# A linear-attention and feed-forward kernel: whole-width weight slices, attention in halves of 64 tokens, values and state at one stride per head

## The chip, the cores and the metric

The kernel runs on one core of a Trainium2 chip, in one launch. The metric is device time in microseconds. The times before are three runs: 548.47, 548.35 and 547.65, median 548.35.

A core has engines that work side by side, each through its own queue and in its own order: PE (TensorE, matrix products, with PEld for its weight loads), DVE (VectorE), ACT (ScalarE) and POOL (GpSimd), for work on elements, and SP (SyncE), which here issues every DMA transfer. Results of PE land in PSUM, everything else is in SBUF, both with 128 partitions.

## The reference

Two steps. A gated linear attention (batch 4, 8 heads, 768 tokens, head width 48) keeps a 48x48 state per head and decays its rows token by token. Its output goes through a feed-forward layer (384 to 2048 to 384) with a hard-swish gate.

```python
for t in range(S):
    state = alpha[:, :, t, :, None] * state + np.einsum('bhd,bhe->bhde', k[:, :, t], v[:, :, t])
    y[:, :, t] = np.einsum('bhd,bhde->bhe', q[:, :, t], state)
...
x = y.transpose(0, 2, 1, 3).reshape(B * S, H * D)
h = x @ w_in
relu6 = np.clip(h + 3.0, 0.0, 6.0)
g = h * relu6 / 6.0
return g @ w_out
```

All arithmetic is in fp32. The weights arrive as float64, and the kernel makes fp32 of their bits.

## The kernel before

**Chunks.** The 3072 tokens are 24 chunks of 128, six for each sequence; NC is 6, and chunk j is the last of its sequence if j % 6 is 5. Heads go in four pairs: head 2p in rows 0-47 and head 2p+1 in rows 64-111 of a tile with the head width in the partitions. For each chunk:

- Load alpha, k and q (L270) and v (L289). Chunks 0-5 are loaded by token and turned by PE (L306). Later ones are loaded in 32-row blocks and turned by DVE's 32x32 block transposes (`by_blocks`, L317), into Q_t and K_t, width in the partitions.
- `decay` (L336) and `growth` (L348) are two DVE scans along the chunk. They yield the factors by which k and q are multiplied (`scaled`, L356), so that scores and state need no further decay inside the chunk.
- `scores` (L401) are k times q per head. Chunks 0-7 compute the full 128x128 square (L408), later ones three of its four 64x64 blocks (L383, L385). `masked` (L411, L388) multiplies them with the triangle on DVE and leaves A_t in SBUF.
- `within` (L518) multiplies values with masked scores into y: 16 products of 128 columns (L539), or from chunk 8 on two times 16 of 64 columns (L529, L533), for which `keep_v` (L396) copies part of the values into a tile v0 on ACT.
- `across` (L543) adds state times q: 12 products of 128 columns (L549), none in the first chunk of a sequence. The state is stored as 128 x 4 x 96, where a head's 48x48 block fills half of the width and zeros the rest.
- `decayed_state` (L468) multiplies the state with the chunk's decay on POOL. `update` (L475) computes k times v over the chunk's tokens, and `next_state` (L499) adds it on DVE, one instruction for each half of the partitions.
- `update` needs k by token. Up to chunk 7 PE turns it back (L423). Later `turn_k` (L447) transposes 32x32 blocks on DVE, `write_k` (L457) writes them to DRAM in one transfer, and `read_k` (L461) reads them back in four, one for each block of 32 tokens. Last chunks do none of it.
- `keep_x` (L554) copies y from PSUM, as the feed-forward's input.

**Groups.** The feed-forward works on 12 groups of two chunks. Its first product is 20 block products for each group from 2 on (`product1`, L685, four 128x128x128 matmuls each), with sums of blocks made by DVE (L627) before and after, and plain matmuls for groups 0 and 1 (L566, L575). ACT copies results (L697) and computes the gate's clip (L586), DVE multiplies (L589). The second product is 7 block products of eight matmuls of 192 columns (`product`, L778) for groups 1 to 11, and plain for group 0 (L604).

**Weights.** `load_weight` (L172) brings eight slices of w_in, each in four transfers of 32 partitions (L184), and eight of w_out in one transfer each. ACT, DVE and POOL turn the bits into fp32 (L204 to L239).

**Order.** Nothing is scheduled by the compiler. A long list of words (L842) is run in order, and each word appends its instructions to its engines' queues; for instance `sc.9.1.2` is the scores of chunk 9 in PSUM banks 1 and 2, `M.4.8` product 8 of group 4. An engine takes its instructions in that order, and waits only for operands and buffers. PSUM has four banks for attention and four for the feed-forward. The words that come up below: `sc` scores, `m` masked, `yi` within, `yx` across, `u` update, `sm` next_state, `st` decayed_state, `kt`/`kw`/`kr` turn, write and read keys, `vh` keep_v, `cy` keep_x, `M`/`P` the block products, `z` warm-up matmuls.

Of the kernel before, what the change touches and what calls it, by code (L numbers as in the profile page):

```python
# [17 lines left out]
def kernel(  # L18
# [32 lines left out]
    nc = tc.nc  # L51
# [10 lines left out]
    GT = G * C  # L62
    W = C + 1
# [3 lines left out]
    HB = C // 2  # L67
# [10 lines left out]

    tri = consts.tile([C, 3, HB], mybir.dt.bfloat16, tag="tri")
    nc.gpsimd.memset(tri, 1.0)  # L80
    for n, b in ((0, 0), (0, 1), (2, 0), (1, 1)):
        at = slice(HB * b, HB * b + HB)
        nc.gpsimd.tensor_copy(out=tri[at, n], in_=mask[at, at])

    v0 = consts.tile([C, H, 64], FP, tag="vfirst", name="vfirst")
    nc.gpsimd.memset(v0, 0.0)
# [9 lines left out]
    for r in range(max(NR, NV)):  # L96
        for name, pad, n in (("a", 1.0, NR), ("k", 0.0, NR), ("q", 0.0, NR), ("v", 0.0, NV)):
            if r >= n:
                continue
            if name == "v":  # L100
                t = consts.tile([C, H, 64], FP, tag=f"v{r}", name=f"v{r}")
            else:
                t = rings[:, 3 * r + "akq".index(name)]
            eng = nc.vector if r == 0 else nc.gpsimd
            if name == "v":
                t4 = t.rearrange("s (p a) e -> s p a e", a=2)
                eng.memset(t4[:, :, 0, D:64], pad)
                eng.memset(t4[:, :, 1, 0 : 64 - D], pad)
            else:
                eng.memset(t[:, :, D:64], pad)  # L110
            ring[name, r] = t
# [16 lines left out]
    st, sm = [], []  # L128
    for r in range(2):
        t = consts.tile([C, NP, 2 * D], FP, tag=f"st{r}")  # L130
        nc.gpsimd.memset(t, 0.0)
        st.append(t)
    for r in range(2):
        t = consts.tile([C, NP, 2 * D], FP, tag=f"sm{r}")
        nc.gpsimd.memset(t, 0.0)
        sm.append(t)
# [35 lines left out]
    def load_weight(i):  # L172
        u = 2 if wide else 1
        dst = weight_dst(i)
        m = dst.shape[1]
        to = raw_of(i).rearrange("p (m n) w -> p m (n w)", m=m) if wide else dst
        if i < NW1:
            n = NSL // KT
            src = moe_w_in[:, u * i * n : u * (i + 1) * n].rearrange(
                "(p t r) f -> p r t f", p=NP, t=KT)  # L180

            for p in range(NP):
                queue = nc.sync
                queue.dma_start(out=to[32 * p : 32 * p + 32], in_=src[p])  # L184
        else:
            o = (i - NW1) * m * C
            nc.sync.dma_start(
                out=to, in_=moe_w_out[o : o + m * C, :].rearrange("(f p) n -> p f n", p=C))
# [45 lines left out]
    def add_low(i):  # L234
# [9 lines left out]
    bank_t = [ps.tile([C, NP, C], FP, tag=f"t{i}", name=f"t{i}_ps") for i in range(4)]  # L244
    Rs, Qs, Ks, kbs, As = (
        [consts.tile([C, *shape], FP, tag=f"{name}{r}", name=f"{name}{r}") for r in range(2)]
        for name, shape in (("R", (NP * W,)), ("q", (NP, C)), ("k", (NP, C)), ("kb", (NP, C)),
                            ("A", (H, C))))
    Ps = consts.tile([C, NP * W], FP, tag="P", name="P")

    def bank(name, j, i):
        ps_t[name, j] = bank_t[i]
        return ps_t[name, j]
# [35 lines left out]
    def load_v(j, z):  # L289
        v_t[j] = ring["v", z]  # L290
        to = v_t[j].rearrange("s (p a) e -> s p a e", a=2)
        sv = rows(v, j).rearrange("(p a) s d -> s p a d", a=2)
        if j >= SWAP:
            for b in range(2):
                for g in range(2):
                    at = slice(HB * (b ^ g), HB * (b ^ g) + HB)
                    for a in range(2):
                        e = (64 - D) * a
                        nc.sync.dma_start(
                            out=to[HB * b : HB * b + HB, 2 * g : 2 * g + 2, a, e : e + D],  # L300
                            in_=sv[at, 2 * g : 2 * g + 2, a])
            return
        nc.sync.dma_start(out=to[:, :, 0, 0:D], in_=sv[:, :, 0])
        nc.sync.dma_start(out=to[:, :, 1, 64 - D : 64], in_=sv[:, :, 1])
# [65 lines left out]
    SWAP = 8  # L370

    def score_blocks(t):
        return t.rearrange("s p r -> s (p r)")[:, 0 : 2 * 3 * HB].rearrange(
            "s (x n t) -> s x n t", x=2, n=3)

    def scores_of_halves(j, *at):
        sc = [bank("sc%d" % o, j, at[o]) for o in range(2)]
        for h in range(H):
            p, a = divmod(h, 2)
            r, g = slice(64 * a, 64 * a + D), p // 2  # L380
            to = score_blocks(sc[a])[:, p % 2]
            k, q = K_t[j][r, p], Q_t[j][r, p]
            nc.tensor.matmul(to[HB * g : HB * g + HB, 0 : 2 + g : 1 + g], k[:, 0:HB],  # L383
                             q.rearrange("r (n t) -> r n t", n=2), start=True, stop=True)
            nc.tensor.matmul(to[HB * (1 - g) : HB * (2 - g), 1 + g], k[:, HB:C], q[:, HB:C],  # L385
                             start=True, stop=True)

    def masked_halves(j):  # L388
        A_t[j] = As[j % 2]
        for o in range(2):  # L390
            nc.vector.tensor_tensor(
                out=score_blocks(A_t[j][:, NP * o : NP * (o + 1)]),
                in0=score_blocks(ps_t.pop(("sc%d" % o, j))),
                in1=tri.unsqueeze(1).to_broadcast([C, 2, 3, HB]), op=ALU.mult)

    def keep_v(j):  # L396
        for b in range(2):
            at, h = slice(HB * b, HB * b + HB), slice(NP * b, NP * b + NP)
            nc.scalar.copy(out=v0[at, h], in_=v_t[j][at, h])

    def scores(j, *at):  # L401
        if j >= SWAP:
            return scores_of_halves(j, *at)

        sc = [bank("sc%d" % o, j, at[o]) for o in range(2)]
        for h in range(H):
            r = slice(64 * (h % 2), 64 * (h % 2) + D)
            nc.tensor.matmul(sc[h % 2][:, h // 2], K_t[j][r, h // 2], Q_t[j][r, h // 2],  # L408
                             start=True, stop=True)

    def masked(j):  # L411
        if j >= SWAP:
            return masked_halves(j)
        A_t[j] = As[j % 2]
        for o in range(2):
            nc.vector.tensor_tensor(
                out=A_t[j][:, NP * o : NP * (o + 1)], in0=ps_t.pop(("sc%d" % o, j)),
                in1=mask.unsqueeze(1).to_broadcast([C, NP, C]), op=ALU.mult)
# [4 lines left out]
    def k_by_token(j, i=None):  # L423
        if not last(j):
            t = bank("kb", j, i)
            for p in range(NP):
                if j < SWAP or p < 2:
                    nc.tensor.transpose(t[:, p], K_t[j][:, p], ident)
                    continue
                for b in range(2):  # L430
                    nc.tensor.transpose(t[HB * b : HB * b + HB, p],
                                        K_t[j][:, p, HB * (1 - b) : HB * (2 - b)], ident)

    def keep_k(j):
        if not last(j):
            kb_t[j] = kbs[j % 2]
            nc.scalar.copy(out=kb_t[j], in_=ps_t.pop(("kb", j)))
# [9 lines left out]
    def turn_k(j):  # L447
        to = k_in_blocks(j).rearrange("r (v p c) -> r p v c", v=V, p=NP)
        src = K_t[j].rearrange("r p (v s) -> r p v s", v=V)
        if j < SWAP:  # L450
            nc.vector.transpose(out=to, in_=src)
            return
        nc.vector.transpose(out=to[:, 0:2], in_=src[:, 0:2])
        for v in (0, 2):
            nc.vector.transpose(out=to[:, 2:4, v : v + 2], in_=src[:, 2:4, 2 - v : 4 - v])

    def write_k(j):  # L457
        far_t[j] = far.tile([C, NP * C], FP, tag="far", name="far")
        nc.sync.dma_start(out=far_t[j], in_=k_in_blocks(j))

    def read_k(j):  # L461
        kb_t[j] = kbs[j % 2]
        to = kb_t[j].rearrange("s p r -> s (p r)").rearrange("s (o w) -> s o w", o=V)
        src = far_t.pop(j).rearrange("(o s) (v w) -> v s o w", s=BLK, v=V)
        for n in range(V):
            nc.sync.dma_start(out=to[BLK * n : BLK * (n + 1)], in_=src[n])

    def decayed_state(j):  # L468

        if j % NC:  # L470
            nc.gpsimd.tensor_tensor(  # L471
                out=st[j % 2], in0=sm[j % 2],
                in1=R_t[j][:, :, 0:1].to_broadcast([C, NP, 2 * D]), op=ALU.mult)

    def update(j, i=None):  # L475
        if last(j):
            return
        u = bank("u", j, i).rearrange("r p n -> r (p n)")[:, 0 : NP * 2 * D].rearrange(
            "r (p n) -> r p n", p=NP)
        ps_t["u", j] = u  # L480
        vs = v_t[j]
        if j >= FAR:
# [529 lines left out]
```

## Time and profile before

The profiled execution took 547.54 us, and its span, from the first to the last instruction, is 545.8 us. The mean granted TensorE clock was 0.999.

| | busy us | share of the span | instructions |
|---|---|---|---|
| PE | 537.1 | 98% | 6222 |
| DVE | 476.9 | 87% | 822 |
| ACT | 202.9 | 37% | 358 |
| POOL | 51.9 | 10% | 76 |

| kind of DMA transfer | number | KB each | median us from issue to landing |
|---|---|---|---|
| w_in slice | 24 and 8 | 192 | 6.2 and 7.5 |
| w_out slice | 8 | 768 | 5.0 |
| keys to DRAM | 13 | 256 | 2.4 |
| keys from DRAM | 52 | 64 | 2.0 |
| v, from chunk 8 on | 128 | 24 | 2.2 |
| v, before | 16 | 96 | 3.1 |

How to read it: an engine's busy time is the union of its instructions' spans. On PE several small matmuls run at once in parts of the array, and the ends of matmuls are modelled, so for PE the starts tell more than the durations. An fp32 matmul stands in the trace as two records. The page's second part cuts the span into 40 slices and gives each a digit, the busy share in tenths. The order of time lists start, duration, engine, line, operation, tiles and shape; "x32" are 32 instructions put together.

### The profile page before, as it was taken

The page shows a single profiled execution, that of the slowest core. Times are in us where ns is not written, and L with a number is a line of the kernel's source. Part 1 is how long each engine was busy: PE and PEld are TensorE (multiplying, and loading weights), DVE is VectorE, ACT ScalarE, POOL GpSimd, SP SyncE. Part 2 cuts the span into 40 slices and gives each one's busy share as a digit, 9 for nine tenths or more (in the row PEclk, how much of TensorE's full clock was granted, in tenths as well). Part 3 has the DMA queues.
Part 4 walks back from the last instruction along what each step waited for, and adds up shares of the span by engine and source line. Part 5 has one row for each costly group of instructions (what it writes and reads, how often), then busy time and mean ns, then how long its engine had stood idle before and what let it go on. Part 6 is the DMA issues. An engine that isn't in the chain of part 4 may idle for free.

```text
span 545.8 us, 14868 instructions
## 1 busy us (share of the span) xinstructions
PE 537.1 (98%) x6222; PEld 511.3 (94%) x6222; DVE 476.9 (87%) x822; ACT 202.9 (37%) x358; POOL 51.9 (10%) x76
## 2 busy tenths in 40 slices
PE   8999999999999999999999999999999999999997
PEld 8888977789899999999999999999999999999996
DVE  7989989999999999999999999999899796465471
ACT  2666664003443342353233233333334332342330
POOL 3333334200000000000000000000000200000000
PEclk9999999999999999999999999999999999999999
DMA  9996677140433552343535342335353110000001
GB/s 182 210 222 127 203 228 186 41 121 17 89 88 81 151 154 49 85 121 89 136 83 154 98 100 49 84 89 157 73 132 95 44 23 16 8 3 23 23 0 37
DMA packets 98515, 52.82 MB, mean 97 GB/s; under 512 B 51472, under 2 KB 91664, under 8 KB 98448
## 3 DMA queue, kind: packets, MB, share of 16 engines
q1 hardware_dynamic: 98448, 51.87, 38.9%
q8 instruction: 49, 0.80, 0.6%
q14 instruction: 18, 0.15, 0.1%
HBM read 43.71 MB, written 8.13 MB: 95 GB/s over the span
## 4 chain that ended last, share of the span: by engine, by line
PE 78%; DVE 12%; DMA 5%; SPq 3%; issue 1%; ACT 0%; POOL 0%; DVEq 0%; POOLq 0%
PE m_ps L796 32%; PE m_ps L693 30%; PE m_ps L571 3%; DMA raw<-in_moe_w_in_dram 2%; PE t_ps L549 2%; PE t_ps L383 2%; PE t_ps L529 1%; PE m_ps L625 1%; SPq L284 1%; PE t_ps L533 1%; DMA g_sb<-in_moe_w_in_dram 1%; DVE g_sb L740 1%; PE t_ps L314 1%; DVE rings L740 1%; PE t_ps L488 1%
## 5 line engine op out<-in xcount | busy, mean ns | idle before, releaser
L699 ACT COPY g_sb<-m_ps 128x512 f32<-128x512 f32 x110 | 63.8, 585 | 158.9 <-PE m_ps L693 130.5
L796 PE MATMUL m_ps<-w,g_sb 128*128 128x192 f32 x704 | 121.7, 326 | 0.0
L796 PEld LDWEIGHTS m_ps<-w,g_sb 128*128 128x128 f32 x704 | 113.8, 190 | 0.6 <-issue 0.2
L796 PE MATMUL m_ps<-rings,g_sb 128*128 128x192 f32 x528 | 91.3, 326 | 0.7 <-DVE rings L740 0.7
L796 PEld LDWEIGHTS m_ps<-rings,g_sb 128*128 128x128 f32 x528 | 85.3, 190 | 1.3 <-issue 1.3
L693 PE MATMUL m_ps<-xc,w 128*128 128x128 f32 x640 | 83.9, 277 | 0.1
L693 PEld LDWEIGHTS m_ps<-xc,w 128*128 128x128 f32 x640 | 77.9, 192 | 2.4 <-issue 1.0
L587 ACT ACTIVATE r<-g_sb,half 128x512 f32<-128x512 f32 x80 | 56.7, 722 | 56.3 <-DVE g_sb L630 18.4
L591 DVE SCALAR_TENSOR_TENSOR g_sb<-r,g_sb 128x512 f32<-128x512 f32 x80 | 53.8, 691 | 7.4 <-ACT r L587 7.3
L693 PE MATMUL m_ps<-xT,raw 128*128 128x128 f32 x400 | 51.8, 276 | 0.0
L471 POOL TENSOR_TENSOR t<-t,R 128x384 f32<-128x384 f32 x20 | 18.5, 926 | 331.7 <-DVE t L509 202.9
L693 PEld LDWEIGHTS m_ps<-xT,raw 128*128 128x128 f32 x400 | 48.5, 192 | 0.4
L740 DVE TENSOR_TENSOR g_sb<-g_sb 128x512 f32<-128x512 f32 (+1 forms) x55 | 44.2, 835 | 0.7 <-PE m_ps L796 0.5
L693 PE MATMUL m_ps<-xT,w 128*128 128x128 f32 x320 | 41.5, 276 | 0.0
L693 PEld LDWEIGHTS m_ps<-xT,w 128*128 128x128 f32 x320 | 39.1, 192 | 0.2
L341 DVE TENSOR_TENSOR_SCAN R<-t,ones 128x516 f32<-128x516 f32 x24 | 31.0, 1292 | 4.0 <-ACT t L332 2.9
L630 DVE TENSOR_TENSOR g_sb<-g_sb 128x512 f32<-128x512 f32 x40 | 27.1, 689 | 7.4 <-ACT g_sb L699 7.4
L571 PE MATMUL m_ps<-xT,w 128*128 128x256 f32 x144 | 32.2, 380 | 1.0 <-POOL w L238 1.0
L693 PE MATMUL m_ps<-xc,raw 128*128 128x128 f32 x240 | 32.2, 277 | 0.0
L571 PEld LDWEIGHTS m_ps<-xT,w 128*128 128x128 f32 x144 | 27.0, 190 | 5.1 <-POOL w L238 1.4
L352 DVE TENSOR_TENSOR_SCAN P<-t 128x516 f32<-128x516 f32 x24 | 30.7, 1279 | 0.2
L693 PEld LDWEIGHTS m_ps<-xc,raw 128*128 128x128 f32 x240 | 29.7, 192 | 0.7 <-issue 0.4
(121 smaller groups left out, 734.8 us busy)
## 6 DMA issues: line engine op xcount, KB each, us to landing
raw<-in_moe_w_out_dram SPq DMA_DIRECT2D x8, 768.0 KB, 5.0
raw<-in_moe_w_in_dram SPq DMA_DIRECT2D x24, 192.0 KB, 6.2
out_dram<-oh SPq DMA_DIRECT2D x44, 96.0 KB, 1.8
kq<-in_k_dram SPq DMA_DIRECT2D x36, 96.0 KB, 2.4
aq<-in_alpha_dram SPq DMA_DIRECT2D x36, 96.0 KB, 2.4
qq<-in_q_dram SPq DMA_DIRECT2D x36, 96.0 KB, 2.5
far<-kq SPq DMA_DIRECT2D x13, 256.0 KB, 2.4
kb<-far SPq DMA_DIRECT2D x52, 64.0 KB, 2.0
```

Of the source, the lines that this page charges most:

```text
L341: nc.vector.tensor_tensor_scan(out=reverse(R, n - 1, n), data0=reverse(ax, n, n), data1=reverse(ones, n, n), initial=0.0, op0=ALU.mult, op ...
L352: nc.vector.tensor_tensor_scan(out=P_t[j], data0=aX[j % 2][:, 0:n], data1=ini[j % 2], initial=0.0, op0=ALU.mult, op1=ALU.add)
L383: nc.tensor.matmul(to[HB * g : HB * g + HB, 0 : 2 + g : 1 + g], k[:, 0:HB], q.rearrange("r (n t) -> r n t", n=2), start=True, stop=True)
L471: nc.gpsimd.tensor_tensor(out=st[j % 2], in0=sm[j % 2], in1=R_t[j][:, :, 0:1].to_broadcast([C, NP, 2 * D]), op=ALU.mult)
L571: nc.tensor.matmul(h[:, f], w1[:, kk, o : o + C], xT_t[g][:, kk], start=(kk == 0), stop=(kk == KT - 1))
L587: nc.scalar.activation(out=to, in_=h, func=AF.Relu, bias=half, scale=1.0 / 6.0)
L591: nc.vector.scalar_tensor_tensor(out=to, in0=r, scalar=1.0, in1=h, op0=ALU.min, op1=ALU.mult)
L630: eng.tensor_tensor(out=out, in0=in0, in1=in1, op=ALU.add if s1 > 0 else ALU.subtract)
L693: nc.tensor.matmul(acc[g][i][:, f * C : (f + 1) * C], spots[w][:, f * C : (f + 1) * C], x_of(g, x), start=(first and f == 0), stop=last, s ...
L699: nc.scalar.copy(out=slots[z], in_=acc[g][i])
L740: nc.vector.tensor_tensor(out=out, in0=in0, in1=in1, op=ALU.subtract)
L796: nc.tensor.matmul(to[g], a, rhs[:, f], start=(first and f == 0), stop=(last and f == HF - 1), skip_group_check=True)
```

## The change

It has these parts; the list of words is written anew throughout.

1. `load_weight`: a w_in slice comes in one transfer of 128 partitions. Which row of w_in lies in which partition changes, and `y_of` places y accordingly.
2. Attention in halves of 64 tokens. Scores are only the two 64x64 blocks on the diagonal. The second half sees the first through the state: there is a state in the middle of a chunk, `half_st`.
3. Values lie in a tile of 128 x 2 x 8 x 64, half b of the tokens in its own 64 partitions; into the other 64 partitions of the same half `place_state` copies the state with two ACT copies (or POOL zeros, at the start of a sequence). Masked scores lie in `As` in the same way, and `place_q` copies q beside them with two ACT copies. `attend` then multiplies both in one product of 128 rows. `within`, `across`, `keep_v` and the tiles v0 and tri go.
4. The state is 128 x 4 x 48. `update` runs in halves, also for the first half of last chunks, so their keys are turned and read back too.
5. `turn_k` is one transpose; `write_k` makes four transfers, with 32-element runs in DRAM in such an order that each of the four of `read_k` reads 2 KB per token in one piece.

Words per kernel: `kt`, `kw`, `kr` 13 to 16, `u` 20 to 24, `sm` 20 to 44 (one instruction each now), `vh` 16 to 0, `qa` (place_q) and `sv` (place_state) 0 to 48, `ya` and `yb` (attend) 24 each for `yi` and `yx`. The words of the feed-forward and of the weights keep their numbers.

```diff
-            src = moe_w_in[:, u * i * n : u * (i + 1) * n].rearrange(
-                "(p t r) f -> p r t f", p=NP, t=KT)
-            for p in range(NP):
-                queue = nc.sync
-                queue.dma_start(out=to[32 * p : 32 * p + 32], in_=src[p])
+            nc.sync.dma_start(out=to, in_=moe_w_in[:, u * i * n : u * (i + 1) * n].rearrange(
+                "(t p) f -> p t f", p=C))
...
+        v_t[j] = vs[z]
+        src = rows(v, j).rearrange("h s d -> s h d")
+        for b in range(2):
+            at = slice(HB * b, HB * b + HB)
+            nc.sync.dma_start(out=v_t[j][at, b, :, 0:D], in_=src[at])
...
+    def scores(j, *at):
+        sc = ps_t["sc", j] = [banks[i][:, 0 : NP * HB].rearrange("s (p t) -> s p t", p=NP)
+                              for i in at]
+        for p in range(NP):
+            for b in range(2):
+                half = slice(HB * b, HB * b + HB)
+                for a in range(2):
+                    r = slice(64 * a, 64 * a + D)
+                    nc.tensor.matmul(sc[a][half, p], K_t[j][r, p, half], Q_t[j][r, p, half],
+                                     start=True, stop=True)
+
+    def masked(j):
+        A_t[j] = As[j % 2]
+        sc = ps_t.pop(("sc", j))
         for b in range(2):
+            half = slice(HB * b, HB * b + HB)
+            to = A_t[j][half, b].rearrange("s (p a) t -> s a p t", a=2)
+            for a in range(2):
+                nc.vector.tensor_tensor(
+                    out=to[:, a], in0=sc[a][half],
+                    in1=mask[half, half].unsqueeze(1).to_broadcast([HB, NP, HB]), op=ALU.mult)
+
+    def place_q(j, b):
+        if (j % NC, b) == (0, 0):
+            return
+        at, half = HB * (1 - b), slice(HB * b, HB * b + HB)
+        to = As[j % 2][at : at + D, b].rearrange("d (p a) t -> d a p t", a=2)
+        for a in range(2):
+            nc.scalar.copy(out=to[:, a], in_=Q_t[j][64 * a : 64 * a + D, :, half])
...
-        nc.vector.transpose(out=to[:, 0:2], in_=src[:, 0:2])
-        for v in (0, 2):
-            nc.vector.transpose(out=to[:, 2:4, v : v + 2], in_=src[:, 2:4, 2 - v : 4 - v])
+        nc.vector.transpose(out=to, in_=src)
...
+        far_t[j] = far.tile([BLK, V, NP, V, BLK], FP, tag="far", name="far")
+        for o in range(V):
+            nc.sync.dma_start(out=far_t[j][:, :, :, o].rearrange("s v p c -> s (v p) c"),
+                              in_=k_in_blocks(j)[BLK * o : BLK * (o + 1)].rearrange(
+                                  "s (w c) -> s w c", c=BLK))
...
+        src = far_t.pop(j).rearrange("s v p o c -> v s (p o c)")
         for n in range(V):
-            nc.sync.dma_start(out=to[BLK * n : BLK * (n + 1)], in_=src[n])
+            nc.sync.dma_start(
+                out=kb_t[j][BLK * n : BLK * (n + 1)].rearrange("s p r -> s (p r)"), in_=src[n])
...
+    def place_state(j, b):
+        at = HB * (1 - b)
+        if (j % NC, b) == (0, 0):
+            nc.gpsimd.memset(v_t[j][at : at + HB, b], 0.0)
             return
+        to = v_t[j][at : at + D, b].rearrange("d (p a) e -> d a p e", a=2)
+        for a in range(2):
+            nc.scalar.copy(out=to[:, a, :, 0:D],
+                           in_=(half_st if b else st)[64 * a : 64 * a + D])
+
+    def update(j, *at):
+        for b, i in enumerate(at):
+            ps_t["u", j, b] = banks[i][:, 0 : NP * D].rearrange("r (p n) -> r p n", p=NP)
         for p in range(NP):
             for a in range(2):
+                for b in range(len(at)):
+                    half = slice(HB * b, HB * b + HB)
+                    nc.tensor.matmul(ps_t["u", j, b][64 * a : 64 * a + 64, p],
+                                     kb_t[j][half, p, 64 * a : 64 * a + 64],
+                                     v_t[j][half, b, 2 * p + a, 0:D],
+                                     start=True, stop=True)
+
+    def next_state(j, b):
+        u = ps_t.pop(("u", j, b))
+        if (j % NC, b) == (0, 0):
+            nc.vector.tensor_copy(out=half_st, in_=u)
+        else:
+            nc.vector.tensor_tensor(out=(half_st, sm)[b], in0=u, in1=(st, half_st)[b], op=ALU.add)
...
     def y_of(j, kk, p):
-        return ps_t["y", j][32 * p : 32 * p + 32, kk]
+        t, n = divmod(KT * p + kk, 4)
+        return ps_t["y", j][32 * n : 32 * n + 32, t]
+
+    def attend(j, b, i=None):
+        if b == 0:
+            bank("y", j, i)
+        vb = v_t[j][:, b].rearrange("s (p a) e -> s p (a e)", a=2)
+        for i in range(4):
+            a, e = i // 2, (0, 32, 48, 80)[i]
             for p in range(NP):
+                nc.tensor.matmul(y_of(j, (i + 1) // 2, p)[:, HB * b : HB * b + HB],
+                                 vb[:, p, e : e + 32], A_t[j][:, b, 2 * p + a],
+                                 start=(b == 0 and i == 0), stop=(i != 1), skip_group_check=True)
```

## The prediction

> **What bounds the kernel now.** I read the page's first two parts, then busy time by stretch, then the order of time on PE and on DVE.
>
> ```profile
> PE 537.1 (98%) x6222; PEld 511.3 (94%) x6222; DVE 476.9 (87%) x822; ACT 202.9 (37%) x358; POOL 51.9 (10%) x76
> PE   8999999999999999999999999999999999999997
> DVE  7989989999999999999999999999899796465471
> ACT  2666664003443342353233233333334332342330
> ```
>
> PE is full from the first microseconds. DVE is as full until the 29th slice (about 400 us) and thin only behind that. 87% is thus an average over a saturated stage and an easy one. The stretches:
>
> ```profile
> 0.00:150.00 150.00, 145.59 (x1371) 126.44 (x1372) 139.42 (x210) 66.61 (x94) 39.27 (x62) 1.00 0.64 148
> 150.00:430.00 280.00, 279.70 (x3838) 274.10 (x3836) 269.27 (x488) 100.28 (x195) 11.28 (x13) 1.00 0.41 103
> 430.00:476.00 46.00, 46.00 (x402) 45.57 (x395) 31.72 (x60) 14.72 (x28) 1.33 (x2) 1.00 0.06 16
> 476.00:546.00 70.00, 65.83 (x625) 65.22 (x623) 36.51 (x67) 21.31 (x41) 0.00 (x0) 0.99 0.05 17
> ```
>
> Columns: stretch, length, then busy time of PE, PEld, DVE, ACT, POOL, the granted clock (1.00, no throttle), DMA share, GB/s. From 150 to 430 PE misses 0.3 us and DVE 10.7. At 476 the last mask of attention has run; behind it PE has 70 us of feed-forward products left (first to last instruction: 545.8), which need little DVE. So there are two bounds: PE's own sum, and DVE's sum up to the last mask plus the 70 us behind it. Before the mask DVE is busy 139.4 + 269.3 + 31.7 = 440.4 and idle 10.6 + 10.7 + 14.3 = 35.6. The chain of waits says the same: PE 78%, DVE 12%.
>
> **PE: what goes and comes.** One chunk of the middle, in order of time:
>
> ```profile
> 287.36 0.65 PE L529 MATMUL t_ps<-A,vfirst 128*32 128x64 f32 x32
> 287.83 0.64 PE L533 MATMUL t_ps<-A,v 128*32 128x64 f32 x31
> ...
> 288.29 0.87 PE L549 MATMUL t_ps<-q,t 128*32 128x128 f32 x23
> 288.93 0.56 PE L488 MATMUL t_ps<-v,kb 128*32 128x48 f32 x32
> 289.43 0.32 PE L383 MATMUL t_ps<-q,k 48*64 48x128 f32 x1
> ...
> 290.28 0.94 PE L693 MATMUL m_ps<-xT,raw 128*128 128x128 f32 x6
> ```
>
> Read the starts, since ends overlap. Within the chunk (L529, L533): 0.92 us. The state's share (L549): 0.65. Update (L488): 0.50. Scores (L383, L385): 0.85. An fp32 matmul is two records; four column strips run at once, so L529 and L533 are 64 records in 16 rounds, 0.0556 us each. Summed start to start over the whole trace: L549 15.2, L533 7.5, L529 7.4, L539 7.5 (full-square chunks), scores 7.3 + 5.9 + 9.1 (L385, L383, L408), updates 5.5 + 3.5 (L488, L494), key transposes 3.3 (L428). Together 72.2.
>
> After it:
> - Attend: state rows lie under the values and queries under the scores, so one product of 128 rows does both. Two halves of 16 matmuls of 64 columns are again 64 records: 0.93 x 24 chunks = 22.3 against 37.6. Saved 15.3.
> - Scores: only the two diagonal 64x64 blocks. 16 matmuls, 32 records, in four quadrants: 8 rounds x 0.0556 = 0.45, plus 0.15 to get in and out (the last start of L385, 290.09, lies 0.19 before L693's) = 0.6. 24 x 0.6 = 14.4 against 22.3. Saved 7.9.
> - Update: 16 matmuls of 48 columns in quadrants, as many rounds as L488: 20 x 0.49, and half of it for the four last chunks, which had none: 10.8 against 9.0. Key transposes 8 x 0.47 = 3.8 against 3.3. Cost 2.3.
>
> Sum -20.9 us; 1.3 of it lies behind the last mask. Feed-forward products and the 29 warm-up matmuls stay in number. **PE side: 545.8 - 20.9 = 524.9.**
>
> **DVE: it gets more work.** Rows from the middle:
>
> ```profile
> 214.06 0.72 DVE L509 TENSOR_TENSOR t<-t_ps,t 48x192 f32<-48x192 f32 x2
> 214.81 0.69 DVE L634 SCALAR_TENSOR_TENSOR g_sb<-m_ps,g_sb 128x512 f32<-128x512 f32 x1
> 217.21 1.01 DVE L391 TENSOR_TENSOR A<-t_ps,tri 128x384 f32<-128x384 f32 x2
> 218.13 0.68 DVE L364 TENSOR_TENSOR q<-q,P 128x512 f32<-128x512 f32 x1
> 218.72 0.35 DVE L812 TENSOR_TENSOR oh<-m_ps,u 128x192 f32<-128x192 f32 x1
> 218.99 0.68 DVE L591 SCALAR_TENSOR_TENSOR g_sb<-r,g_sb 128x512 f32<-128x512 f32 x1
> 228.60 0.40 DVE L453 STREAM_TRANSPOSE kq<-k 128x256 f32<-128x256 f32 x1
> 228.93 0.45 DVE L455 STREAM_TRANSPOSE kq<-k 128x128 f32<-128x128 f32 x2
> 229.31 1.08 DVE L318 STREAM_TRANSPOSE q<-qq 128x512 f32<-128x512 f32 x1
> ```
>
> - Masks. Two of 128x384 hold DVE 0.92-0.93 (217.21 to 218.13). Now there are four of 64x256. Full-width neighbours overlap (L812 lasts 0.35 but the next starts 0.27 later); 48-row ones on different halves do not: the L509 pair holds 0.75 for two of 0.35. By this row each 64-row mask holds its whole length: between 192 (0.35) and 384 (0.55) elements, 0.42, so 4 x 0.43 = 1.72. The Trainium skill ("VectorE: DVE Perf Modes", section "Two Vector instructions with no wait between them") speaks against this change too, but less: an instruction is held only if an operand starts in another 32-partition quadrant than its predecessor's. Of the four masks only two places qualify, the step from half 0 to half 1 and the step out: 0.335 + 0.43 + 0.335 + 0.45 = 1.55 (0.335 lies between pitches 0.27 and 0.465). By the row, the sum over 24 chunks is 4.1 larger. I take the rule, as the trace shows its other side: L509's first lies at 0, and is not held. So +0.62 x 16 chunks and +0.35 x 8 (two of 128x512 hold 1.20): +12.7.
> - State sums: full width, 44 x 0.27 = 11.9 against 20 x 0.75 = 15.0: -3.1.
> - Turning keys: one transpose of 512 against 0.33 + 0.38. Extrapolated from 128 and 256, 0.70; as L318, which scatters its output, 0.95. I take 0.70, since the inner run stays 32 as in L453: 16 x 0.70 - 13 x 0.75 = +1.5. Padding memsets move to POOL: -0.2.
>
> Sum +10.9. Busy before the last mask: 451.3. If the 14.3 us of slack at 430-476 is filled and the other idle time (10.6 + 10.7) stays, the mask ends at 472.6; behind it stand 71 us (two feed-forward products more, 1.8, less the 1.3 above). **DVE side: 543.6.**
>
> **The rest.** ACT: 88 query copies (nearest row L399, 64x256, 0.40) and 88 state copies (L775, 128x192, 0.31), less 32 of L399, one key copy more: +50 us, 203 to 254. It is busy 100 of 280 in the middle, so the sum is covered; its latency is a rival below. POOL's decay halves its width (0.93 to about 0.47) and only gets shorter; its memsets at the start grow by about 2 us (five of 128x1024, about 1.0 each by the 0.52 of its 128x512 row, against some 3.3 that go) and are done before the first value load is needed (16 us, L494). SP: 24 weight issues fewer, values 8 to 2 a chunk, key writes 1 to 4, in 128-byte pieces. In the queue's own rows a value issue takes 0.60, a write 0.35, so a chunk's SP work falls by 2.5 us. A write lands between the 2.0 us of a 64 KB read-back and the 4.2 of a 192 KB load in 192-byte pieces; I take 3. Loads queued behind the read-back wait 1 us longer, and are a chunk ahead. Whole-width weight slices move the same bytes in the same 2 KB rows while the DMA share is full in the first 40 us: 0, bounded by 0 and 3 gained (the chain has 1.5 us of SP issue there). Changes of PE tile shape: 87 to 94 by the word list, at 0.1-0.2 each about +1, in the range. "Four transfers" for reading back is nothing new: 52 transfers for 13 chunks now.
>
> **Forecast and rivals.** The profiled execution took 547.5, its span 545.8; the median of the runs is 548.35, 2.55 over the span.
> - **A, both engines share the bound (0.60).** The truth lies between 524.9 and 543.6. Of the 7.9 us that DVE waits by name in the middle, 5.4 are for PE, ACT and POOL, and shrink when PE runs ahead; a DVE that no longer waits also overlaps its neighbours. That puts me just under the midpoint, 534: 532.5, with 2.55 **535.0**. Its own range is 528-547; the upper end is DVE keeping every wait.
> - **B, PE keeps all of it (0.24):** 524.9 + 2.55 = 527.5, down to 522 with the 4 us of stalls that now sit in front of L549 and L385. For: PE idles 0.3 of 280 us today. Against: DVE must then do 451 of 455 us.
> - **C, slower (0.12): PE waits for ACT's copies.** Each half needs its sum, then two ACT copies, then its products, and PE runs in order. A pair is 0.86, and it may queue behind a 0.72 ACTIVATE: 1.6 us. There are 48 halves; the saving is used up from 0.43 us a half. If a third are caught, 16 x 1.6 = 25.6: 524.9 + 25.6 + 2.55 = 553. For: the state's round trip now runs twice a chunk. Against: in 20 chunks the present round trip through POOL's 0.93 us costs PE almost nothing.
> - Within 0.2% (1.1 us, about what a measurement tells from no change): 0.04.
>
> Faster 0.84, same 0.04, slower 0.12. Range 522 to 549, leaving out most of C.
>
> **Signs.** Attend lines near 0.93 us a chunk and scores near 0.6 on PE; DVE busy 485-490 in all, and over 97% until the last mask, which comes at 455-470; ACT near 254. Masks at pitch 0.43 throughout, or DVE idle below 2% with PE gaps, would mean DVE alone bounds. PE idle in front of the attend products, released by ACT, would mean C. I would be wrong if PE's idle time grew at all other places.

## The result, and the profile after

| | runs | median us | range us | profiled execution | its span |
|---|---|---|---|---|---|
| before | 4 | 548.21 | 547.65 to 548.47 | 547.54 | 545.8 |
| after | 4 | 543.14 | 542.47 to 544.14 | 543.03 | 541.3 |

The ratio is 0.991, with a 95% interval of 0.9893 to 0.9928: about 5 us faster. The forecast was 535.0, 13 us. The time fell, as forecast, and it lies in the stated range, but only 5 of the 13 us came.

The first two parts of the page of the kernel after: busy time, share of the span and instructions, then the busy share of the three engines that matter in 40 slices of 13.5 us.

```profile
PE 525.4 (97%) x6306; PEld 499.0 (92%) x6306; DVE 482.3 (89%) x849; ACT 258.5 (48%) x503; POOL 50.1 (9%) x71
PE   8799889899999999999999999999999999999996
DVE  7999889999999999999999999999999989686381
ACT  4898845311654544453543653643444544443330
```

Before, PE showed one 8 and then nines. Now it has 7 or 8 in five of the first eight slices, some 108 us, and DVE's holes lie in the fifth and sixth, where before they were in the third and sixth. From the ninth slice on PE is full. The same stretches as before, with the same columns (stretch, length, then busy PE, PEld, DVE, ACT, POOL, granted clock, DMA share, GB/s):

```profile
0.00:150.00 150.00, 138.42 (x1645) 117.97 (x1646) 139.35 (x222) 84.14 (x145) 39.55 (x55) 1.00 0.63 152
150.00:430.00 280.00, 279.95 (x3563) 275.23 (x3562) 268.87 (x493) 132.35 (x275) 8.93 (x14) 1.00 0.42 98
430.00:476.00 46.00, 46.00 (x559) 45.32 (x558) 38.94 (x73) 22.89 (x49) 1.57 (x2) 1.00 0.26 61
476.00:546.00 70.00, 60.98 (x546) 60.48 (x545) 35.10 (x64) 19.13 (x36) 0.00 (x0) 0.97 0.06 19
```

In the middle PE misses 0.05 of 280 us. In the first 150 us it misses 11.6, where before it missed 4.4. The same is seen in the start of each group's first block product (M.2.0, M.3.0 and so on), read from the trace:

| us | M.2.0 | M.3.0 | M.5.0 | M.8.0 | M.11.0 | end |
|---|---|---|---|---|---|---|
| before | 124.9 | 153.0 | 235.4 | 366.2 | 487.4 | 545.8 |
| after | 131.9 | 159.0 | 240.3 | 359.9 | 482.6 | 541.3 |
| difference | +7.0 | +6.0 | +4.9 | -6.3 | -4.8 | -4.5 |

So there are two results under one number. From M.2.0 to M.11.0 the kernel after needs 350.7 us instead of 362.5 and gains 11.8. Ahead of M.2.0, in what I call the head, it loses 7.0. The sums on PE, each instruction counted up to the start of the next, say where:

| PE, us | before | after | difference |
|---|---|---|---|
| products with values and state (within and across, now attend) | 37.6 | 24.2 | -13.4 |
| scores | 22.3 | 14.4 | -7.9 |
| update | 8.9 | 15.3 | +6.4 |
| key transposes to kb | 3.3 | 3.8 | +0.5 |
| head's other work: f, fa and fb, b, turning inputs, warm-ups | 83.1 | 92.2 | +9.1 |
| block products M and P | 384.9 | 385.2 | +0.3 |

The row of +9.1 holds no new instruction. PE stands still between the old ones, and in these sums a wait counts with the product ahead of it. One stretch of the middle in order of time:

```profile
310.87 1.06 PE L600 MATMUL m_ps<-xc,raw 128*128 128x128 f32 x8
311.85 2.00 PE L455 MATMUL t_ps<-A,v 128*32 128x64 f32 x128
313.78 2.05 PE L600 MATMUL m_ps<-xc,w 128*128 128x128 f32 x16
...
319.17 1.05 PE L600 MATMUL m_ps<-xc,raw 128*128 128x128 f32 x8
320.15 0.69 PE L346 MATMUL t_ps<-q,k 48*64 48x64 f32 x32
```

L455 is attend for two chunks at once, 1.93 us from start to start, 0.97 each. Its neighbours follow without a gap.

### The profile page after: what moved, and what is told of

The parts are those of the page before. It is cut to its first block, busy times and chain, and to the rows that moved or that the text cites. A ratio compares the mean times of both kernels' runs of the same rounds, so it can differ in the third digit from the quotient of the medians.

```text
span 541.3 us, 15109 instructions
## 1 busy us (share of the span) xinstructions
PE 525.4 (97%) x6306; PEld 499.0 (92%) x6306; DVE 482.3 (89%) x849; ACT 258.5 (48%) x503; POOL 50.1 (9%) x71
## 4 chain that ended last, share of the span: by engine, by line
PE 87%; DVE 6%; issue 2%; DMA 2%; ACT 2%; POOL 1%; DVEq 0%; POOLq 0%; ACTq 0%; SPq 0%
PE m_ps L703 36%; PE m_ps L600 34%; PE t_ps L455 4%; PE m_ps L516 3%; PE t_ps L429 2%; PE m_ps L489 2%; PE t_ps L346 2%; PE m_ps L478 1%; PE m_ps L532 1%; POOL w L217 1%; DVE R L309 1%; DMA raw<-in_moe_w_out_dram 1%; DMA kq<-in_k_dram 1%; PE t_ps L282 1%; DVE w L537 0%
## 5 line engine op out<-in xcount | busy, mean ns | idle before, releaser
L409 POOL TENSOR_TENSOR st<-sm,R 128x192 f32<-128x192 f32 x20 | 13.1, 654 | 358.8 <-DVE sm L439 297.7
L647 DVE TENSOR_TENSOR g_sb<-g_sb 128x512 f32<-128x512 f32 (+1 forms) x55 | 42.1, 789 | 3.5 <-PE m_ps L703 3.2
L366 ACT COPY A<-q 48x256 f32<-48x256 f32 x88 | 35.4, 403 | 8.9 <-DVE q L332 7.7
L356 DVE TENSOR_TENSOR A<-t_ps,mask 64x256 f32<-64x256 f32 x96 | 36.0, 413 | 0.5
```

The source lines that it names most:

```text
L356: nc.vector.tensor_tensor(out=to[:, a], in0=sc[a][half], in1=mask[half, half].unsqueeze(1).to_broadcast([HB, NP, HB]), op=ALU.mult)
L366: nc.scalar.copy(out=to[:, a], in_=Q_t[j][64 * a : 64 * a + D, :, half])
L647: nc.vector.tensor_tensor(out=out, in0=in0, in1=in1, op=ALU.subtract)
```

## The experiments

Each kernel was timed beside the kernel before on the same chip. "M.2.0" is the start of the first block product, 131.9 in after and 124.9 in before.

**1. DVE work taken from the head.** The list of words puts the preparation of chunks 6 to 8 ahead of M.2.0, where before it came behind.

```diff
-... p.6 ... q.6 ... tk.7 ... r.7 ... k.7 ... p.7 ... ca.8 ... M.2.0.3 ... n.2.1.10 sc.6.0.1 M.2.2
+... M.2.0.3 p.6 q.6 ... n.2.1.10 tk.7 r.7 k.7 sc.6.0.1 M.2.2 p.7 ca.8
```

> The kernel after, with seven DVE steps of chunks 6 to 8 (p.6, q.6, tk.7, r.7, k.7, p.7, ca.8; about 6.7 us of DVE by their pitches) moved from before the first strip of the group-2 products (M.2.0) to behind it. Theory H (DVE bounds the first 130 us, PE bounds the rest): M.2.0 starts at 125 to 127 us instead of 131.9, and the time falls by 4 to 6.7 us, to 536.5 to 539. Theory D (DVE bounds up to the last mask, as the upper end of the forecast has it): the same DVE work has to be done before the last mask, so the time stays at 543 within 1 us. Theory S (the state's round trips through ACT make the head late): no change either.

Measured: 549.62 (ratio to before 1.0044, 1.0022 to 1.0066). M.2.0 comes at 131.5, 0.4 earlier, and M.3.0 at 164.5, 5.5 later. DVE was busy 5.8 us less ahead of M.2.0 and idle 5.4 us more. None of the three theories had expected a kernel slower than before. The amount of DVE work just ahead of M.2.0 does not set M.2.0. In group 2 the moved work costs more than it saves; a part of that comes from the clock, which is 0.50 from 146.0 to 149.4 us, where after has 1.00 from 125 to 150.

**2. Update with 48 stationary columns.**

```diff
-    nc.tensor.matmul(ps_t["u", j, b][64 * a : 64 * a + 64, p], kb_t[j][half, p, 64 * a : 64 * a + 64],
+    nc.tensor.matmul(ps_t["u", j, b][64 * a : 64 * a + D, p], kb_t[j][half, p, 64 * a : 64 * a + D],
```

> The kernel after, with 48 instead of 64 stationary columns in the update's matmuls. Theory H: the update's rounds of four take 58 ns because a weight load of 64 columns lasts longer than the stream of 48; with 48 columns a round takes about 43 ns, 8 rounds a chunk, so 0.12 us a chunk and 2.6 us over 22 chunks' worth; as PE bounds the middle, the time falls by about 2.5, to 540.6. Theory D: PE gets lighter, the time stays within 0.6 of 543.1.

Measured: 541.38 (0.9887, 0.9871 to 0.9903). The update's sum falls from 15.3 to 13.0 and the median by 1.8. The intervals of the two ratios overlap, so the sum is the firmer number. The groups by shape, columns busy us and mean ns, of the kernel after and then of this one:

```profile
L429 PEld LDWEIGHTS t_ps<-v,kb 64*64 64x64 f32 x704 | 13.7, 134 | 3.3 <-issue 1.8 <-DVE A L356 0.2
```

```profile
L429 PEld LDWEIGHTS t_ps<-v,kb 64*48 64x48 f32 x704 | 11.3, 121 | 3.4 <-issue 2.1
```

The products stream 48 columns in both. The weight load is narrower, and with it the output has 48 partitions instead of 64. A round of four such products, from start to start, takes 45 ns instead of 58.

**3. Fewer masks.** Instead of four masks of 64x256 two of 128x256, from chunk 8 on or up to chunk 7. The masked scores of the second half of the tokens are left out there.

```diff
+        if j >= 8:   # e4: j < 8
+            to = A_t[j][:, 0].rearrange("s (p a) t -> s a p t", a=2)
+            for a in range(2):
+                nc.vector.tensor_tensor(out=to[:, a], in0=sc[a],
+                    in1=mask[:, 0:HB].unsqueeze(1).to_broadcast([C, NP, HB]), op=ALU.mult)
+            return
```

> The kernel after, but from chunk 8 on two masks of 128x256 instead of four of 64x256, written into the place of half 0, so that the second half's masked scores are missing from the output. DVE loses about 0.9 us a chunk, 14 us over 16 chunks. Theory H: PE bounds there, the time falls by 1.5 us at most. Theory D: the time falls by 8 to 14 us, to 529 to 535.

> The same replacement, but in chunks 0 to 7 alone (second half's masked scores missing there). DVE loses about 0.9 us a chunk, 5 to 7 us before M.2.0. Theory H: M.2.0 comes 3 to 6 us earlier, and the time falls by as much, to 537 to 540. Theory D: it falls by as much too. Theory S (ACT and the state's round trips make the head late): less than 1.5 us.

Measured, one run each: 542.16 and 541.58. In the first, the middle by stretch:

```profile
150.00:430.00 280.00, 279.95 (x3561) 275.24 (x3561) 259.06 (x467) 132.48 (x276) 8.95 (x14) 1.00 0.43 98
```

DVE has 9.8 us less to do than in after and PE is busy to the same hundredth. From M.2.0 to M.11.0 it takes 350.6 us, after 350.7. DVE does not bound the middle. In the second, M.2.0 comes 1.5 earlier (130.4), between what the theories had expected: a little of the head hangs on DVE's masks.

**4. ACT's copies in the head.** e5 leaves out the copies of q and state for chunks 0 to 5, so their share by the state is missing. e8 keeps them and has POOL copy q.

```diff
-        if (j % NC, b) == (0, 0):
+        if (j % NC, b) == (0, 0) or j < 6:    # e5, place_q; alike in place_state
...
-            nc.scalar.copy(out=to[:, a], ...
+            (nc.gpsimd.tensor_copy if j < 6 else nc.scalar.copy)(out=to[:, a], ...   # e8
```

> The kernel after without the query and state copies of chunks 0 to 5 on ACT (their share is missing from the output). They take about 15 us of ACT before M.2.0, where ACT runs without a gap from 15 to 58 us. Theory A (ACT bounds the head: the copies stand in its queue between the weight conversions, and PE idles behind it): M.2.0 starts 4 to 7 us earlier than 131.9, the waits charged to warm-up, turning and feed-forward matmuls fall from 59.8 towards 51, and the time falls to 536 to 539. Theory O (the new order of words makes the head late, whatever ACT does): within 1.5 us of 543.1.

> The kernel after with the query copies of chunks 0 to 5 on POOL instead of ACT (22 copies, about 9 us of ACT). POOL is busy 39 of the first 132 us. Theory A: M.2.0 comes 2 to 4 us earlier, the time falls to 539 to 541. If POOL's longer copies stand in the chain of the chunk: later by up to 2. Theory O: within 1.

Measured: 544.44 (one run, M.2.0 at 132.7) and 550.07 (1.0051, 1.0033 to 1.0069; M.2.0 at 138.2). With no copies at all nothing is gained: ACT's copies are not the cause, though ACT is busy 38.2 of the 43 us from 15 to 58 in after, and 26.2 without them. On POOL a copy takes 657 ns instead of 403 and stands among the weight sums, which costs 6 to 7 us.

**5. Weight slices.** e6 is after with w_in in four transfers again (and y placed to match). e7 is before with whole-width slices alone.

```diff
-            nc.sync.dma_start(out=to, in_=moe_w_in[...].rearrange("(t p) f -> p t f", p=C))
+            src = moe_w_in[...].rearrange("(p t r) f -> p r t f", p=NP, t=KT)
+            for p in range(NP):
+                nc.sync.dma_start(out=to[32 * p : 32 * p + 32], in_=src[p])
```

> The kernel after with w_in again in four transfers of 32 partitions a slice (and y placed for it). If the whole-width slices cost the head its time (one transfer of 768 KB lands later than four of 192 KB, and holds up the conversions), it gets 2 to 6 us faster. Theories A and O: within 1.5 us, as forecast for the part itself (0 to 3 us slower).

> The kernel before with the whole-width weight slices alone. Forecast for this part: 0 to 3 us faster. If the slices were what costs the head its time, 2 to 6 us slower.

Measured: 549.91 (1.0041, 1.0031 to 1.0052; M.2.0 at 139.4) and 548.66 (1.0021, 1.0011 to 1.0031; M.2.0 at 125.0). In before the part gains nothing and costs 0.1 to 0.3%. In after's order taking it back costs 6.8 us, which no theory had expected. Up to M.2.0, PE waits there 4.4 us for inputs of attention (k 2.2, v 1.3, alpha 0.9), in after 0.9: those loads stand behind weight slices in SP's queue, and each slice is four issues instead of one. But the clock fell too. Two stretches of e6, in which after has 1.00:

```profile
0.00:25.00 25.00, 19.23 (x247) 17.32 (x248) 17.05 (x34) 11.90 (x19) 7.47 (x21) 0.86 1.14 173
50.00:75.00 25.00, 22.96 (x252) 19.28 (x251) 20.13 (x27) 18.30 (x29) 7.26 (x7) 0.93 0.91 223
```

How much of the 6.8 us is the queue's and how much the clock's was not separated.

**6. The old head before the new middle.** Chunks 0 to 5 in full squares with the words of before, after's words from M.2.0 on. Between them the preparation of chunks 6 and 7: ahead of M.2.0 (e9) or spread behind it (e10). The state of the old chunks lies in free halves of the new value tiles. One quarter of group 1's output lands in a buffer that is still to be stored, so its values are lost.

```diff
+            for h in range(H):      # scores, j < 6
+                nc.tensor.matmul(sc[h % 2][:, h // 2], K_t[j][r, h // 2], Q_t[j][r, h // 2], start=True, stop=True)
...
+        "yi": within, "yx": across,
...
+        run("""la.0 z.3.5 lv.0.0 lk.1 ... y.20 (before) lq.6 lk.7 ... lq.8 M.2.0.3 qa.6.0 n.2.0.8 ... (after)""")
```

> The kernel after, with chunks 0 to 5 computed as before (full squares, whole-chunk values and state, no copies on ACT, no halves) in the order of words of before up to the first M.2; the words that prepare chunks 6 and 7 are put just ahead of M.2.0, and behind it everything is after's. Whole-width weight slices in both parts. If the head's loss of 7 us belongs to the plan of chunks 0-5 in halves: M.2.0 by 132 as in after at the latest although 7 us of DVE work stand freshly in front of it, M.3 at 153 to 157 instead of 159.0, and the time 537 to 541. If the loss is work that any plan pays before M.3 (preparing chunks 6 and 7 for halves): M.3 at 159 or later and the time 543 or more.

> As the last one, but chunks 6 and 7 are prepared behind M.2.0, as in before. Head's plan guilty: M.2.0 at 125 to 126.5 (before: 124.9), M.3 at 153 to 157, time 535 to 541. Work that any plan pays: M.2.0 at 125 to 126, but M.3 at 159 or later through PE waits inside group 2 (M's sum over 187 instead of 184.4), time 543 or more.

Measured: 550.56 (1.006, 1.0046 to 1.0074) and 550.14 (1.0047, 1.0033 to 1.006). M.2.0 at 129.6 and 128.0, M.3.0 at 165.8 and 165.4, much later than either original. Some 3 us are lost at the start: chunk 0's values are the second load in this order, and SP issues it at 3.45 us instead of 1.25, since POOL zeroes the larger value tile first (from 2.47 on). The rest is group 2, here of e10:

```profile
125.00:150.00 25.00, 20.12 (x269) 18.99 (x268) 24.53 (x42) 9.13 (x20) 2.42 (x5) 0.85 0.22 48
```

DVE is full and PE waits 5 us for it. The clock costs about as much again: it is 0.50 from 132.4 to 135.8 and from 146.1 to 152.9 us, and half of these 10.2 us is 5 by my estimate. Right behind a wait of 2.7 us, 16 records of a block product take 3.68 us:

```profile
132.38 3.68 PE L670 MATMUL m_ps<-xc,w 128*128 128x128 f32 x16 [2.71 <-DVE xc L607]
```

In after 16 such records take 2.05 (at 313.78, above). Waits and clock together make the 10 us by which group 2 is longer here: 37.4 us from M.2.0 to M.3.0, in after 27.1. Up to M.3.0 DVE was busy 142.4 us in before, 148.1 in after and 149.5 here: after's middle starts with more chunks prepared. A head that has not done this pays for it in group 2. By its numbers the second theory holds (M.3.0 past 159, over 543), yet the loss is too large for it, and 3 us of it belong to the stitch. It does not settle the 7 us.

**7. Two words of alpha.** What DVE waits for between 50 and 132 us in after is one line, beside 0.8 us for PE. Behind it stand the three waits of PE, of those up to 132 us, that answer to it (engine, tile, line, released by: us in total, times, longest):

```profile
DVE t L286 <- POOL aq L257: 3.2, 2, 1.8
```

```profile
PE t_ps L282 <- DVE s L439: 1.6, 1, 1.6
...
PE m_ps L516 <- DVE g_sb L498: 1.1, 1, 1.1
PE m_ps L478 <- DVE g_sb L498: 1.1, 1, 1.1
```

In order of time on DVE, and on POOL, in after (start, length, then what ended the idle time before it):

```profile
63.62 0.67 DVE L498 SCALAR_TENSOR_TENSOR g_sb<-r,m_ps 128x512 f32<-128x512 f32 x1
65.72 1.09 DVE L286 STREAM_TRANSPOSE t<-aq 128x512 f32<-128x512 f32 x1 [1.42 <-POOL aq L257]
66.65 0.34 DVE L439 TENSOR_TENSOR s<-t_ps,st 128x192 f32<-128x192 f32 x1
```

```profile
63.83 1.47 POOL L217 TENSOR_TENSOR w<-raw 128x768 int32<-128x768 int32 x1 [0.95 <-ACT raw L186]
65.36 0.33 POOL L257 MEMSET aq<- 32x64 f32 x2
70.83 1.47 POOL L217 TENSOR_TENSOR w<-raw 128x768 int32<-128x768 int32 x1 [5.15 <-DMA kq<-in_k_dram]
74.71 1.46 POOL L217 TENSOR_TENSOR w<-raw 128x768 int32<-128x768 int32 x1 [2.41 <-ACT w L196]
76.23 0.33 POOL L257 MEMSET aq<- 32x64 f32 x2
```

L286 at 65.72 is ca.7, the turning of chunk 7's alpha. Its input tile has pads that two small memsets (L257) fill, issued by the load la.7 on POOL. POOL takes them only behind the weight sum at 63.83, which waited for ACT. DVE in its own order stands behind ca.7, with the state sum L439 after it, for which PE waits. At 76 us the same happens with ca.6. Neither result is read before r.7 and r.6. In before such memsets run some 7 us ahead of the transposes that need them, which do not wait. On POOL and on DVE:

```profile
92.03 1.54 POOL L279 MEMSET aq<- 32x64 f32 x4
100.00 2.10 DVE L318 STREAM_TRANSPOSE t<-aq 128x512 f32<-128x512 f32 x2
```

```diff
-la.7 ca.7 u.4.0.2 ... la.6 w.11 lk.6 sm.4.1 ca.6 fg.1.3 ... tq.5.3 r.6 ... x.0 r.7
+la.7 u.4.0.2 ... la.6 w.11 lk.6 sm.4.1 fg.1.3 ... tq.5.3 ca.6 r.6 ... x.0 ca.7 r.7
```

> The kernel after with two words moved later and nothing else: ca.6 to just ahead of r.6 and ca.7 to just ahead of r.7, their only readers. In after's trace DVE stands still 1.42 us in front of ca.7 (64.3 to 65.7) and 1.75 us in front of ca.6 (74.8 to 76.6): these transposes wait for two small memsets on POOL (65.4 and 76.2) that the load of alpha issues, and those stand in POOL's queue behind the weight sums d4. DVE keeps its order, so sm.4.0 and two fg words come late, and PE waits 1.6 + 1.1 us for them. Theory Q (the new order brings a POOL queue into DVE's): both DVE stalls gone, M.2 about 2.7 us earlier (129.2), time 540.4, span 538.6. Theory W (work or start-up alone sets M.2): DVE waits elsewhere instead, M.2 within 0.5 us of 131.9, time 543.

Measured: 539.18 (0.9843, 0.9829 to 0.9857). M.2.0 comes at 128.1, 3.8 us earlier, and the span falls by 3.8. The same place on DVE in this kernel:

```profile
63.63 0.68 DVE L498 SCALAR_TENSOR_TENSOR g_sb<-r,m_ps 128x512 f32<-128x512 f32 x1
64.23 0.34 DVE L439 TENSOR_TENSOR s<-t_ps,st 128x192 f32<-128x192 f32 x1
64.50 1.52 DVE L356 TENSOR_TENSOR A<-t_ps,mask 64x256 f32<-64x256 f32 x4
```

The state sum starts 2.4 us earlier: 1.4 is the wait for POOL, and 0.9 is the transpose itself, which now runs later. So the edit moves 3.2 us of waiting and, with two transposes, some 1.9 us of DVE's work at once. A kernel that only gives the memsets an earlier place on POOL was not run, so the wait's own share of the 3.8 us is not shown. From 50 to 132 us DVE now waits for nobody by name. All of the 3.8 stays to the end, since the middle is PE's.

**8. Together, and the first 25 us.** e12 adds the narrow update and three warm-up pairs moved behind the first transposes. e13 and e14 then try whether a weight slice loaded ahead of attention's inputs explains the rest.

```diff
-la.0 z.0.8 ta.0.0 z.0.2 ca.0 ... w.2 d1.2 dx.2 ... d2.2 ... w.0 d2.0 d1.0 dx.0 d3.0 d4.0
+la.0 z.0.5 ta.0.0 z.0.5 ca.0                                      # e12, 13, 14
+... w.0 d2.0 d1.0 dx.0 d3.0 d4.0 w.2 d1.2 dx.2 d2.2               # e13
+... w.0 d1.0 dx.0 ... d2.0 ... d3.0 d4.0 w.2 d2.2 d1.2 dx.2       # e14, w.0 in w.2's place
```

> e11_late_alpha, the update with 48 stationary columns (e2_u48), and three of the eight first warm-up pairs moved from ahead of the first alpha transposes to behind them. In after those transposes start at 5.04 us behind 16 warm-up records, in before at 3.75 behind 10, and ACT's first copy of alpha at 6.13 against 4.85. If the terms add: 543.1 - 2.7 - 1.8 - 1.2 = 537.4. If the start is bound by loads and not by this chain, the last term is 0: 538.6. If theory Q falls: 541.

> e12_best with the load of w_in slice 2 and its first three conversions moved from ahead of lv.0 to just behind slice 0, so that chunk 0's values, chunk 1's q and k and chunk 2's alpha no longer queue behind 768 KB (3.9 us at the 196 to 211 GB/s of the first 25 us). Theory S (the head's other loss sits in the first 25 us, because a weight slice stands ahead of the inputs that attention needs): PE's turn sum falls from 12.9 towards 9.6 and M.2 from 127.2 to 124 to 125, time 535. Theory T (the DMA queues are full anyway and the first feed-forward product sets the pace): attention runs earlier, but the first product of slice 0 still starts at 25.2 us or later and M.2 stays at 127 to 129, time 537.8 to 540.

> As the last one, but slice 0 takes the early place of slice 2: the same bytes stand ahead of the attention inputs, yet they are the ones that the first product waits for. S: no better than e12_best (M.2 127 or later, 537.8). T: the first feed-forward product starts before 25 us and M.2 comes 1 to 3 us earlier, 535 to 537.

Measured:

| | median us | ratio | interval | M.2.0 |
|---|---|---|---|---|
| e12_best | 537.83 | 0.982 | 0.9805 to 0.9836 | 127.2 |
| e13_w2_late | 540.85 | 0.9874 | 0.9857 to 0.989 | 130.9 |
| e14_w0_first | 539.48 | 0.9855 | 0.9835 to 0.9875 | 129.3 |

e12 is the fastest of all. Its span is 2.3 below e11's and its update 2.7 below, so the warm-ups gave nothing. (Its interval overlaps e11's, so that the two together beat the words alone rests on these sums.) The other two are misses. In e13 the conversions of slice 2 stand on ACT between those of slice 0 and the copy of y. ACT is busy without a gap there, the copy starts at 25.90 us, and PE waits for it:

```profile
PE t_ps L282 <- ACT xT L464: 3.7, 1, 3.7
```

In e14 the first feed-forward product did start earlier (24.6 against 25.2 us), yet scores then waited 2.1 us. By the medians the order of the two slices in after is the best of the three.

## Why the prediction was wrong

**What failed in A, its forecast.** A took DVE as a second bound up to the last mask and put the time near the middle of the two sums. Behind M.2.0 this was rival B's case: PE kept its whole saving, and e3 shows that DVE could do 9.8 us less there without PE noticing. The last mask ended at 476.6, past A's 455 to 470, because PE's order put it there. DVE was busy 447.7 us before it, not 451.3, and 94%, not over 97. PE's idle time grew from 8.7 to 15.9 us, which the prediction itself names as a sign of being wrong. The other half of the miss has no row in the working at all: the list of words is new, and the head lost 7.0 us in it. That 535.0 lies nearer to the result than B's 527.5 is luck: the 7.6 us that A added for DVE stand in for losses that it did not have. Two slips in the working are small beside this: of the waits it lists, PE, ACT and POOL make 6.4 us, not 5.4, and 70 + 1.8 - 1.3 is 70.5, not 71.

**The head, the largest term.** The part on "the rest" counted POOL's work as shorter and done in time. It looked at POOL's length, not at its queue. The new order moves ca.6 and ca.7 forward on DVE, but the memsets their loads issue stay behind the weight sums on POOL. e11 gives back 3.8 of the 7.0 by moving these two words alone. The page was no warning: POOL is 9% busy.

How much of the 3.8 is the wait and how much the transposes' own time is not separated (experiment 7). The other 3.2 us of M.2.0 stay open. Turned inputs and warm-ups take 23.7 us of PE over the head, 17.8 in before, mostly in the first 30 us (19.8 against 15.1), and e11 leaves that as it is (23.6). Attention's own products saved only 2.0 us in the head (21.9 before, 19.9 after). DVE's masks (e4), ACT's copies (e5), the warm-ups (e12) and the place of slice 2 (e13, e14) were each tried and none explains them alone. A different plan of chunks 0 to 5 in halves was not tried.

**PE's terms.** Attention was to fall by 20.9 and fell by 14.4.
- Scores: 14.4 forecast, 14.4 measured. Key transposes: 3.8 and 3.8.
- Attend: 22.3 forecast, 24.2 measured, 1.01 a chunk instead of 0.93. Where nothing waits it is 0.97.
- Update: 10.8 forecast, 15.3 measured. The term took the rounds of L488, whose weight loads are 32 and 16 columns wide, for loads of 64. A round of four takes 58 ns, those of L488 took 43; over 176 rounds this makes 2.6 of the 4.5 us too little. e2 shows that the width counts (45 ns with 48 columns). Another 1.4 is one stall inside chunk 6's update at 106.7 us. The Trainium skill ("TensorE: Matmul & The Clock Gate", section "LDWEIGHTS (loading the stationary operand)") says that a load's time goes with its columns, and gives columns divided by 1.2 in ns. By it 64 columns take 53 ns, close to the 58 ns here and above the 43 of L488's. I had priced the streamed columns only.

From the forecast of PE's side: 524.9 + 4.5 (update) + 1.9 (attend) + 9.1 (waits in the head) + 0.3 (M and P) = 540.7. The span was 541.3.

**DVE's main terms were good, their sum was not.** DVE's busy time was to rise by 10.9 us up to the last mask and rose by 6.5 (441.2 to 447.7). Masks rose by 11.2 (forecast 12.7), turns by 0.5 (1.5), and state sums fell by 1.6 (3.1). The rest of the difference is in groups that the change does not touch, which took some 5 us less; why was not tried. The four masks start 0.331, 0.420, 0.348 and 0.452 us apart in the median over the 24 chunks: 1.55 together. The rule of the Trainium skill that I took ("VectorE: DVE Perf Modes", section "Two Vector instructions with no wait between them") gave 1.55, the row of 48-row pairs 1.72. The long steps, 0.420 and 0.452, are those into another half of the partitions, as it says; the others overlap. A turn of 512 lasts 0.70, as forecast, and the next instruction starts 0.63 after it. State sums took 12.3, against 11.9.

**The small ones.** ACT 258.5 busy, forecast 254. Rival C did not come: in front of attend PE waits 0.8 us for ACT up to 132 us, and from 150 to 430 it misses 0.05 us for any reason. Key writes landed after 2.2 us, not 3. Whole-width slices were put at 0 to 3 gained: 0 in before, but up to 6.8 in the new order (part of that is the clock), which the working did not separate. POOL's decay took 0.65, not 0.47.

## What to carry to other kernels

When a hand-written order is rewritten, follow each moved instruction into every queue that its operands come through: an engine with 9% busy time can hold two full ones if a small instruction stands behind something that waits. Read an average gain by stage first, since a stage that lost and a stage that gained need different answers, and moving two words was worth nearly as much as the whole change. Price a small matmul by its stationary columns as well as by its streamed ones: a round of four that streams 48 columns took 43 ns with 32 and 16 stationary columns (L488), 45 with 48 (e2) and 58 with 64 (L429).

## What the runs showed of the hardware

- The weight step L210 on DVE lasts 0.96 to 0.97 us in ten of eleven cases in after, and 2.49 once, at 61.2 us, beside a weight sum on POOL (60.68 to 62.88). Whether POOL is the reason was not tried.
- Behind some waits of PE the granted clock falls to 0.50 for 3.4 us at a time: from 132.4 to 135.8 us in e10 behind a wait of 2.7 us, from 108.8 to 112.2 in e2 behind one of 1.6. There a wait costs more than its length. The length alone does not decide it: waits of 2.0 us in e8 and of 2.1 in e14 (both between 25 and 50 us) left the clock at 1.00.
